# Reordering stores, weight packing, LayerNorms and product chains in a Strassen-type transformer kernel

## The chip, the cores and the metric

The kernel runs on one core of one Trainium2 chip. The metric is the device time of one execution in microseconds (us). Each execution is listed with the granted TensorE clock, the share of its full speed that TensorE was let have. A profile is of one execution; its span is some 1.7 us shorter than the time of that execution.

## The reference, cut to what matters

```python
x = A_x                                     # (1, 2048, 1024) bf16
x = x + A(layernorm(x), wqkv, wo)           # linear attention: 32 heads, phi(t) = t+1 or exp(t), num / den, then wo
x = x + B(layernorm(x), w_gate, w_up, w_down)
x = x + A(layernorm(x), wqkv, wo)           # the same weights a second time
x = x + B(layernorm(x), w_gate, w_up, w_down)

def B(x, w_gate, w_up, w_down):             # F = 3584
    return ((x @ w_gate) * (x @ w_up)) @ w_down
```

## The kernel before

All large products are Strassen-type: TensorE multiplies sums and differences of blocks, and VectorE makes those sums and combines the products. A recording helper, `P.add(engine, ...)`, puts each operation on one of five engines. **Each engine takes its operations in the order in which they are given to it**, and the semaphore waits follow from what the operations read and write. In the profile's names `arena` is the on-chip memory, `ps` a bank in which TensorE accumulates, and a name ending in `scratch` a buffer in the chip's main memory. All transfers are issued by SyncE (`sp`), so there is one in-order queue of them: a transfer that must wait for its data holds up all that stand behind it. (The prediction shows a case: eight stores are issued from 955.38 us on, and the transposes behind them only from 961.44.)

The stages, with their times before: first attention 0 to 186 us, its output stage (`y_grp`, L1232) to 241, first gate/up pass to 416, down to 501, second gate/up pass to 666, down to 753; then the same again: attention 753 to 917, output stage to 979, gate/up to 1136, down to 1224, gate/up to 1382, down to 1470. The first block must make the sums of the weights. It *packs* weight columns into a scratch buffer, makes the sums and stores them; the second block only loads them.

A gate/up pass takes 14 pairs of weight units. The order of work inside a pair is a string:

```python
ORDER0 = "D3A' P5B' R0 51 D4B' T0 P1A D3B' 56 P1B P6A R0 T1 D2A P6B P7A P5A 57 S5+ D2B P7B D4A"
ORDER1 = "D4A' P5B' 11 D3A' 51 16 D4B' D2B' T1 R0 P1A 17 D3B' P6A 56 S5+ T0 P1B 41 D2A 57 R0 P6B S2+ 46 P7A P5A 47 P7B"
```

`P1A` is product 1 of unit A on a PSUM bank, `D2`, `D3`, `D4` are last products and the multiplication, `51`, `56`, `57` are steps of a second Strassen level inside product 5, and `'` means "of the pair before". `R0` issues the next load of the ring of weight buffers. `T0` and `T1` are ticks, where other work is hooked in. `S5+` and `S2+` are the sums of weights for the next pair: the first block makes them on VectorE and stores them, the second block loads them.

The hooks that the change touches:

```python
def pack():                                  # two transfers of 256 KB, 256 bytes at a time
    ...
    for i in range(2):
        dma(w16[:, i], wgu_v[m][:, :, c0:c0 + 128], ...)

def stash(i):                                # store a part of the residual x
    dma(xscr[i * 128:(i + 1) * 128, :], x_res[:, i, :], ...)

# output stage of the attention block, item i of 16
for i in range(NST):
    ...                                      # normalization, ring loads
    nxt.b1_one()                             # LayerNorm of the next block, in steps
    y_grp(tok[i], 0, i)
    y_seed(i + 1)                            # ScalarE copies the residual into PSUM ahead of its products
    nxt.b2_one()
    y_grp(tok[i], 1, i)
    if not first and i == 9:
        for k in range(8):
            stash(k)

# second attention block: finish one LayerNorm per item from item 1 on
elif n >= 1:
    ...
    job(n, 0, lnp.flush_b)
    job(n, 2, lnp.flush_a)

# hooks of the first gate/up pass and of its down product
def ticks0(u):
    if u % 2 == 0 and not lnp.done():
        lnp.flush_step()                     # a LayerNorm
    if first and u:
        wd_tick(u)                           # down weights: load, sums, store
    if first and u % 2 == 0:
        pack()
```

## Time and profile before

| | us |
|---|---|
| time, median of 4 runs | 1478.07 (1476.38 to 1478.68) |
| span of the profile | 1473.8 |
| TensorE busy | 1442.5 (98%) |
| TensorE's starts beyond the matmuls' own pace | 42.6 |

The last row is the useful one. It is worked out in the prediction: the distance between the starts of two matmuls, less the time that the first needs at full pace. The page's part 4 follows back what released the last instruction, and who released that, as shares of the span by engine:

```profile
PE 74%; DVE 11%; DMA 9%; issue 2%; ACT 2%; POOL 1%; SPq 1%; DVEq 0%; ACTq 0%; POOLq 0%
```

A quarter of the chain that ended last is not TensorE, although TensorE is busy 98%. The view of waits says which transfers VectorE waited for (total us, how many times, the longest):

```profile
DVE arena L757 <- DMA arena<-in_B_w_down_dram: 21.3, 12, 6.7
DVE arena L757 <- DMA arena<-w_scratch: 13.7, 9, 2.3
```

The first are the down weights in the first gate/up pass, the second the ring loads in the second pass.

### The profile page before, as it was taken

What the parts mean: (1) busy time and instruction counts of PE and PEld (TensorE: products, weight loads), DVE (VectorE), ACT (ScalarE), POOL (GpSimd) and SP (SyncE); (2) the same over time, 40 slices, a digit from 0 to 9 for tenths busy, and PEclk for the clock granted to TensorE, in tenths of its full rate; (3) what the DMA queues carried; (4) which work ended last, traced back from release to release, by engine and by line L of the source; (5) the groups of instructions that cost most, each with busy time, mean ns of one, the idle gap of its engine ahead of it and who ended that gap; (6) DMA issues with size and microseconds to landing.
All of it is one profiled execution on the core that took longest, in us unless ns stands there. A gap on an engine that the chain in (4) does not pass through costs nothing.

```text
span 1473.8 us, 21078 instructions
## 1 busy us (share of the span) xinstructions
PE 1442.5 (98%) x7850; PEld 755.0 (51%) x7850; DVE 1126.3 (76%) x2248; ACT 655.9 (45%) x1354; POOL 138.9 (9%) x176
## 2 busy tenths in 40 slices
PE   8999999999999999999999999999999999999999
PEld 3444444445544466554444444446666445666544
DVE  6987878888854698887579878778888636888842
ACT  5672345444410165551037823557776004777400
POOL 2203521000000000001010045210000000000000
PEclk9999999999999999999999999999999999999999
DMA  7478966999866766777884167668775856777652
GB/s 257 87 200 229 216 135 155 276 313 305 282 219 212 244 236 236 236 254 255 269 271 129 51 171 162 170 154 275 262 259 189 305 180 218 263 263 257 211 192 96
DMA packets 270456, 320.18 MB, mean 217 GB/s; under 512 B 161936, under 2 KB 212880, under 8 KB 270352
## 3 DMA queue, kind: packets, MB, share of 16 engines
q1 hardware_dynamic: 270352, 318.82, 70.9%
q8 instruction: 62, 1.02, 0.3%
q14 instruction: 42, 0.34, 0.1%
HBM read 236.45 MB, written 73.40 MB: 210 GB/s over the span
## 4 chain that ended last, share of the span: by engine, by line
PE 74%; DVE 11%; DMA 9%; issue 2%; ACT 2%; POOL 1%; SPq 1%; DVEq 0%; ACTq 0%; POOLq 0%
PE ps L1596 23%; PE ps L1310 21%; PE ps L1391 14%; PE ps L1130 6%; PE ps L911 6%; DMA arena<-w_scratch 3%; DVE arena L757 3%; DMA arena<-arena 3%; PE ps L882 3%; DVE arena L443 2%; DMA arena<-in_B_w_down_dram 2%; DVE arena L1007 1%; SPq L416 1%; DVE arena L1004 1%; PE ps L1232 1%
## 5 line engine op out<-in xcount | busy, mean ns | idle before, releaser
L757 DVE TENSOR_TENSOR arena<-arena 128x512 f16<-128x512 f16 (+10 forms) x951 | 432.4, 480 | 96.1 <-ACT arena L1395 32.4
L760 DVE SCALAR_TENSOR_TENSOR arena<-ps,arena 128x512 f16<-128x512 f32 (+2 forms) x497 | 334.3, 686 | 175.1 <-PE ps L1596 151.3
L1310 PE MATMUL ps<-arena 128*128 128x512 f16 x1888 | 459.2, 380 | 5.6 <-DVE arena L760 5.1
L1596 PE MATMUL ps<-arena 128*128 128x512 f16 (+1 forms) x1568 | 340.9, 379 | 0.0
L1391 PE MATMUL ps<-arena 128*128 128x256 f16 x2184 | 289.8, 273 | 8.7 <-ACT arena L1395 4.8
L1310 PEld LDWEIGHTS ps<-arena 128*128 128x128 f16 (+1 forms) x1888 | 183.5, 98 | 170.3 <-DVE arena L760 9.3
L1391 PEld LDWEIGHTS ps<-arena 128*128 128x128 f16 (+1 forms) x2184 | 211.3, 98 | 102.6 <-ACT arena L1395 14.0
L1596 PEld LDWEIGHTS ps<-arena 128*128 128x128 f16 x1568 | 153.4, 98 | 183.1
L1315 ACT ACTIVATE arena<-ps 128x512 f32<-128x512 f32 x224 | 134.1, 598 | 61.4 <-PE ps L1310 49.0
L1339 ACT COPY ps<-ps 128x512 f32<-128x512 f32 x112 | 65.4, 584 | 182.2 <-PE ps L1310 172.7
L1395 ACT ACTIVATE arena<-ps 128x256 f32<-128x256 f32 x351 | 125.3, 385 | 24.4 <-PE ps L1391 20.1
L911 PE MATMUL ps<-arena 128*128 128x512 f16 (+1 forms) x560 | 123.2, 379 | 3.3 <-ACT arena L918 1.2
L1401 ACT COPY ps<-ps 128x256 f32<-128x256 f32 x182 | 65.8, 362 | 135.3 <-DVE ps L1404 73.9
L1232 PE MATMUL ps<-arena 128*128 128x512 bf16 x512 | 113.0, 383 | 4.0 <-ACT ps L1226 4.0
L1130 PE MATMUL ps<-arena 128*128 128x512 bf16 x512 | 116.1, 379 | 0.0
L443 DVE BATCH_NORM_STATS2 arena<-arena 128x6 f32<-128x512 bf16 x128 | 88.3, 689 | 11.9 <-DMA arena<-in_A_x_dram 6.9
L1013 POOL TENSOR_TENSOR arena<-arena 128x1024 f16<-128x1024 f32 x32 | 75.5, 2358 | 189.5 <-DVE arena L1011 172.2
L911 PEld LDWEIGHTS ps<-arena 128*128 128x128 f16 x560 | 53.9, 98 | 71.6 <-ACT arena L918 5.4
L882 PE MATMUL ps<-arena 128*128 128x512 bf16 x384 | 85.5, 379 | 4.0 <-ACT arena L547 1.6
L1232 PEld LDWEIGHTS ps<-arena 128*128 128x128 f16 x512 | 50.2, 99 | 66.4 <-ACT ps L1226 5.4
L446 POOL TENSOR_SCALAR arena<-arena 128x1 f32<-128x1 f32 x64 | 20.3, 317 | 659.8 <-DVE arena L445 659.8
L1404 DVE TENSOR_TENSOR ps<-ps,arena 128x256 f32<-128x256 f32 x182 | 77.8, 428 | 2.6 <-PE ps L1391 2.6
(56 smaller groups left out, 750.5 us busy)
## 6 DMA issues: line engine op xcount, KB each, us to landing
arena<-w_scratch SPq DMA_DIRECT2D x84, 896.0 KB, 4.9
arena<-t_scratch SPq DMA_DIRECT2D x32, 896.0 KB, 5.9
arena<-in_B_w_down_dram SPq DMA_DIRECT2D x24, 896.0 KB, 5.5
arena<-sp_scratch SPq DMA_DIRECT2D x26, 768.0 KB, 4.4
w_scratch<-arena SPq DMA_DIRECT2D x28, 512.0 KB, 5.6
arena<-w_scratch SPq DMA_DIRECT2D x28, 384.0 KB, 4.7
x_scratch<-arena SPq DMA_DIRECT2D x40, 256.0 KB, 7.6
arena<-x_scratch SPq DMA_DIRECT2D x40, 256.0 KB, 5.7
```

What stands on the lines that cost most here:

```text
L443: P.add("dve", (lambda h: lambda e: e.bn_stats(st[j][:, 6 * h:6 * h + 6], x_res[:, i, (D // 2) * h:(D // 2) * (h + 1)]))(h), rd=r_x(i, (D ...
L757: P.add("dve", lambda e: e.tensor_tensor(out=out, in0=a, in1=b, op=op), rd=rd, wr=wr, prd=prd)
L760: P.add("dve", lambda e: e.scalar_tensor_tensor(out=out, in0=a, scalar=sc, in1=b, op0=ALU.mult, op1=op1), rd=rd, wr=wr, prd=prd)
L882: return [e.matmul(psb(bank), xnT[:, k, i * 128:(i + 1) * 128], t[:, k, h * 512:(h + 1) * 512], start=(k == 0), stop=(k == KT - 1)) for k ...
L911: P.add("pe", lambda e: [e.matmul(psb(bank), a[0][:, k, :], b[0][:, k, :], start=(q in (1, 5) and k == 0), stop=(k == 3), skip_group_check ...
L1130: return [e.matmul(psb(bank), xrt[t][:, jj * 128:(jj + 1) * 128], pk[:, h, t, :], start=(t == tok[0]), stop=(t == tok[NST - 1])) for t in ts]
L1232: return [e.matmul(psb(bank), xnT[:, g, i * 128:(i + 1) * 128], wp[:, g, dh * 512:(dh + 1) * 512], start=(dh == 0 and g == 0), stop=(g == ...
L1310: P.add("pe", lambda e: [e.matmul(psb(bank), w[:, k, :], x[:, k, :], start=(start and k == 0), stop=(k == 3), skip_group_check=True) for k ...
L1315: P.add("act", lambda e: e.activation(t, psb(bank), AF.Copy, scale=SG), prd=[bank], wr=r)
L1391: P.add("pe", lambda e: [e.matmul(psb(bank)[:, 256 * half:256 * half + 256], w[:, k, :], xx[:, k, :], start=(start and k == 0), stop=(k == ...
L1395: P.add("act", lambda e: e.activation(d, src, AF.Copy, scale=sc), prd=[xk], wr=rd_)
L1596: P.add("pe", lambda e: [e.matmul(psb(bank), hv[:, 7 * hf + k, t * 128:(t + 1) * 128], w[:, k, :], start=(q in "15" and hf == 0 and k == 0 ...
```

## The change

The intent is to keep what TensorE waits for from standing behind late transfers. It adds and removes no matmul. The core of the diff:

```diff
-    ORDER0 = "D3A' P5B' R0 51 D4B' T0 P1A D3B' 56 P1B P6A R0 T1 D2A P6B P7A P5A 57 S5+ D2B P7B D4A"
-    ORDER1 = "D4A' P5B' 11 D3A' 51 16 D4B' D2B' T1 R0 P1A 17 D3B' P6A 56 S5+ T0 P1B 41 D2A 57 R0 P6B S2+ 46 P7A P5A 47 P7B"
+    ORDER0 = "D3A' P1A P7B' P6A D2B' 51 D4B' D3B' R0 56 D2A P1B T0 P7A 57 P5A W P6B T1 D4A R0 P5B S5+"
+    ORDER1 = "P5A' 47' T0 P7B' D4A' P5B' 11 D3A' R0 51 16 D4B' D2B' P1A 17 T1 56 D3B' P6A P1B 41 R0 57 S5+ S2+ D2A P6B 46 P7A"
 ...                                         # second attention block
-                elif n >= 1:
+                elif n >= 2:
 ...                                         # output stage
+                if first and i % 3 == 1:
+                    pack()
 ...
-                if not first and i == 9:
-                    for k in range(8):
-                        stash(k)
+                if not first and i >= 8:
+                    stash(i - 8)
 ...                                         # head of a gate/up pass
-                pre = ("P1A", "P1B") + (("P5A", "P5B") if l2 else ())
+                pre = ("P1A", "P1B") + (("D2A", "D2B") if jit else ()) + ("P5A", "P5B")
 ...
+                early = not first
+                if early:
+                    for q in "25":
+                        sums(1, q)           # the next pair's sums are loaded first of all
 ...
             def ticks0(u):
-                if u % 2 == 0 and not lnp.done():
-                    lnp.flush_step()
-                if first and u:
-                    wd_tick(u)
+                if first and u % 2:
+                    wd_next()                # sums only; the token W issues the loads and stores
                 if first and u % 2 == 0:
                     pack()

             def dticks0(q, t):
-                if q == "2" and t == 3:
-                    for k in range(8):
-                        stash(8 + k)
+                if q in "12" and not lnp.done():
+                    lnp.flush_step()         # LayerNorms now under the down product
+                if q in "26":
+                    stash(8 + 4 * "26".index(q) + t)
```

Cut here: the operand sums of the first pair are now made one per token, and `wd_tick` is split into `wd_dma` (load and store) and `wd_next` (sums).

More of the change, by code (lines that the diff above doesn't have):

```diff
@@ L1496, in gateup, with tp_next @@
                 n0 = ps_ * NPASS
-                pre = ("P1A", "P1B") + (("P5A", "P5B") if l2 else ())
+                pre = ("P1A", "P1B") + (("D2A", "D2B") if jit else ()) + ("P5A", "P5B")
                 tpl = tp_ops(ps_, l2)
-                early = [(q, f) for q in dict.fromkeys(tk[0] for tk in order if tk[0] in l2) for f in tpl[q][:3]]
-                def b12(q):
-                    for x in [x for x in early if x[0] == q]:
-                        x[1]()
-                        early.remove(x)
-                    tpl[q][3]()
+                todo = [(q, k) for q in dict.fromkeys(tk[0] for tk in order if tk[0] in l2) for k in range(4)]
+                plain = set()
+                def tp_next(q0=None):
+                    for q, k in list(todo):
+                        if (q == q0) if q0 else (k < 3 or q in plain):
+                            assert k < 3 or q in plain
+                            todo.remove((q, k))
+                            tpl[q][k]()
+                            if not q0:
+                                return
                 def emit(p, tk, head=False):
@@ L1512, in emit @@
                         return
+                    if p == 1 and tk[0] in l2 and tk[1] == "1":
+                        tp_next(tk[0])
                     c, x = pairs[p], "AB".find(tk[-1])
@@ L1522, in emit @@
                             ring_issue()
-                    elif tk[0] == "S":
+                    elif tk == "W":
+                        wd_dma()
+                    elif tk[0] == "S" and not (early and p == 0):
                         sums(p + (tk[2] == "+"), tk[1])
-                    else:
+                    elif tk[0] == "T":
                         i = int(tk[1])
@@ L1532, in emit @@
                     if p == 0 and tk in ("P1B", "P5B", "D2B", "D4B") and tk[1] in l2:
-                        b12(tk[1])
+                        plain.add(tk[1])
+                    if p == 0 and not head:
+                        tp_next()
                 if jit:
@@ L1542, in gateup @@
                         emit(p, tk)
-                        if p == 0 and early:
-                            early.pop(0)[1]()
                 late = [tk for tk in order if tk[-1] == "'"]
@@ L1642, in layer_B, with wd_dma, wd_next @@
             if first:
-                def wd_tick(u):
-                    j = u // 2
-                    if u % 2:
-                        wd_prep(j)
-                    else:
-                        if j:
-                            wd_store(j - 1)
-                        if j < NJ:
-                            wd_load(j)
+                wd = dict(load=0, prep=0, store=0)
+                def wd_dma():
+                    if wd["store"] < wd["prep"]:
+                        wd_store(wd["store"])
+                        wd["store"] += 1
+                    if wd["load"] == wd["prep"] and wd["load"] < NJ:
+                        wd_load(wd["load"])
+                        wd["load"] += 1
+                def wd_next():
+                    if wd["prep"] < wd["load"]:
+                        wd_prep(wd["prep"])
+                        wd["prep"] += 1
             def ticks0(u):
-                if u % 2 == 0 and not lnp.done():
-                    lnp.flush_step()
-                if first and u:
-                    wd_tick(u)
+                if first and u % 2:
+                    wd_next()
                 if first and u % 2 == 0:
@@ L1661, in dticks0 @@
             def dticks0(q, t):
-                if q == "2" and t == 3:
-                    for k in range(8):
-                        stash(8 + k)
+                if q in "12" and not lnp.done():
+                    lnp.flush_step()
+                if q in "26":
+                    assert q == "2" or lnp.done()
+                    stash(8 + 4 * "26".index(q) + t)
                 if q == "5":
@@ L1710, in layer_B @@
             if first:
-                wd_tick(0)
+                wd_dma()
             tail = gateup(0, ticks0, L2SETS[not first, 0])
-            if first:
-                wd_tick(2 * NJ)
-            lnp.need(NST - 1)
+            while first and wd["store"] < NJ:
+                wd_next()
+                wd_dma()
             tq = t_ops(1)
```

## The prediction

> **What bounds the kernel now.** I read the page first, part 1: TensorE is busy almost all the span.
>
> ```profile
> PE 1442.5 (98%) x7850; PEld 755.0 (51%) x7850; DVE 1126.3 (76%) x2248; ACT 655.9 (45%) x1354; POOL 138.9 (9%) x176
> ```
>
> The change alters no matmul, so the matmul work is a floor, and all there is to win is TensorE's waiting. A busy share hides short waits (a group's mean 512-column matmul "lasts" 379 ns, but in the chain of waits 378 of them take 81.58 us, 0.2158 us each), so I went through the trace's matmul start times and took 0.2158 us per 512 columns (0.109 per 256, from 14 in 1.53 us) off each step. What is left over is 42.6 us in the whole span: 10.4 us before 100 us, which the change does not touch, 1.3 at 184 us, 28.5 us in nine places after 240 us, and crumbs. That is 1.9% of 1478.1, so a gain over 2% is nearly out of reach.
>
> Then the table of stretches, cut at the stages. Its columns are the stretch, its length, busy time of PE, PEld, DVE, ACT, POOL with counts, the granted clock, the DMA share and GB/s.
>
> ```profile
> 241.00:258.00 17.00, 13.95 (x60) 5.96 (x59) 16.04 (x41) 6.55 (x12) 1.80 (x4) 0.92 0.87 236
> 306.00:330.60 24.60, 24.42 (x130) 12.41 (x129) 21.57 (x55) 11.58 (x23) 0.00 (x0) 1.00 1.01 326
> 501.00:666.50 165.50, 160.59 (x1005) 97.09 (x1004) 142.06 (x324) 98.21 (x229) 0.00 (x0) 1.00 0.73 244
> 753.50:796.00 42.50, 40.25 (x184) 17.29 (x183) 38.40 (x95) 30.08 (x56) 5.06 (x12) 1.00 0.71 203
> 917.00:979.00 62.00, 58.03 (x262) 25.56 (x260) 43.34 (x84) 32.12 (x45) 14.01 (x28) 0.97 0.65 173
> ```
>
> The first is the entry of the first gate/up pass: VectorE is busy 16.04 of 17 us and TensorE waits for it. The second lies in the same pass: DMA is full (1.01). The third is the first block's second gate/up pass, the fourth the second block's first projections, the fifth its output stage. Last, the timeline says who ends the waits (start, length, engine, line; in brackets the idle time and its releaser):
>
> ```profile
> 254.35 1.15 PE L1310 MATMUL ps<-arena 128*128 128x512 f16 x4 [2.63 <-DVE arena L760]
> ...
> 302.60 1.55 DVE L757 TENSOR_TENSOR arena<-arena 128x512 f16<-128x512 bf16 x4 [1.99 <-DMA arena<-in_B_w_down_dram]
> ...
> 588.56 1.02 DVE L757 TENSOR_TENSOR arena<-arena 128x256 f16<-128x256 f16 x4 [2.17 <-DMA arena<-w_scratch]
> ...
> 591.16 0.39 PE L1391 MATMUL ps<-arena 128*128 128x256 f16 x2 [1.12 <-ACT arena L1395]
> ...
> 761.03 0.55 DVE L463 TENSOR_SCALAR arena<-arena 128x1024 f16<-128x1024 bf16 x1 [1.55 <-DMA arena<-arena]
> ...
> 955.38 6.03 SPq L416 DMA_DIRECT2D x_scratch<-arena  x8
> 961.44 20.00 SPq L531 DMA_TRANSPOSE arena<-arena  x7
> 966.06 1.24 ACT L460 ACTIVATE arena<-arena 128x1024 f16<-128x1024 bf16 x1 [6.37 <-DMA arena<-arena]
> ...
> 968.44 10.49 PE L1232 MATMUL ps<-arena 128*128 128x512 bf16 x40 [2.36 <-ACT ps L1226]
> ...
> 1234.12 0.61 PE L1391 MATMUL ps<-arena 128*128 128x256 f16 x4 [1.81 <-DMA arena<-sp_scratch]
> ```
>
> All follow one pattern: an in-order engine (VectorE, ScalarE or the one DMA queue) is stuck on a late transfer, and what TensorE needs stands behind it.
>
> **What the Trainium skill says.** "TensorE: Matmul & The Clock Gate", section "Back-to-back issue gap": a warm matmul takes N/2.4 + 2.5 ns, 215.8 ns at 512 columns; the trace's 0.2158 us agrees. Its section "What's actually happening" says an idle window of about 3.4 us drops the array to half clock until about 3.4 us of activity. Here the waits of 2.79 us (before 254.35) and 2.53 us (before 968.44) are each followed by steps of 0.427 us, costing 1.6 us more; the wait of 1.77 us at 952.09 is not. So waits above about 2.5 us count extra. "Perfetto Trace Analysis", section "Identifying the Most-Contended Engine", warns that matmul busy share is no measure of distance to the limit; agreed, 31.3 us idle hide 42.6. "DMA: Bandwidth & Descriptors", section "Why small descriptors are slow (HBM only)", puts 27% overhead on 256-byte descriptors. The weight packing moves 128 bf16 columns at a time, that is 256 bytes; the page counts 161936 packets under 512 B, and the passes with packing are those at DMA share 1.0.
>
> **The change part by part** (waits before, my estimate after, all in us):
>
> 1. *Entry of the first gate/up pass, 5.1 to 1.8.* Before: 0.59 + 2.79 waited, 1.6 at half clock. VectorE had 16 weight-sum ops (6.06), a LayerNorm (0.54 + 1.42 + 0.21) and 8 more sums (2.98) ahead of the 0.68 us op that TensorE awaited until 254.29. The change drops the LayerNorm (2.2), puts two product groups (D2A, D2B, 2 x 0.86) ahead of P5, and puts the pair's second sums and the down sums (3.0) behind that op. It should then run near 249.5, when D3A' comes at 241.4 + 10 x 0.863 = 250.0. The next pair's step 51 then waits for about 1.5 + 1.5 + 1.0 us of sums, some 1 to 2 us.
> 2. *Down weights in that pass, 1.95 to 1.2* (0.73, 0.68, 0.34, 0.20 at 292, 305, 317, 377 us). VectorE waited 21.3 us for these loads in all. In the new order a pair's load stands behind its packing in the queue (2.5 us of issue), but the op that needs it comes 9.9 us after D3A' and not 5.5. Packing ends at pair 5, not 10, as five of 28 packs go to the output stage; from there I expect no wait. *Handover to down, 1.35 to 0.7.*
> 3. *Packing in the first output stage, 0 to 1.3, a loss.* Each of the five pairs of transfers is 0.5 MB in the same queue as the LayerNorm transposes. The one beside two ring loads (near 214 us) puts 1.3 to 2 us of issue before a transpose that now takes 5.31 us and that ScalarE already awaits (0.77 idle at 219.67). The seed copies ScalarE makes there finish only 0.2 to 0.7 us ahead of need.
> 4. *First block's second gate/up pass, 6.2 to 2.0* (eight waits of 0.26 to 1.39). The sums of the next pair wait for a ring load (13.7 us on VectorE in all), and the step behind them, 57, waits too. The new order moves these sums from 4.3 to 5.4 us after the load's issue and behind step 57. The load takes 5.9 to 7.0 us, so some wait stays.
> 5. *LayerNorm one item later, 3.0 to 1.3.* It removes VectorE's wait of 1.55 us at 761.03 and delays 2.2 us of work.
> 6. *Stores one by one, 4.1 to 0* (2.53 and 1.6 at half clock). The eight stores took the queue for 6.03 us and held up the transposes that ScalarE awaited for 6.37. The wait of 1.77 at 952 us comes from two ring loads of 0.9 MB, and stays.
> 7. *Entry of the second block's gate/up, 1.95 to 0.9.* Two LayerNorms of 2.2 us leave VectorE. But the sums' load now stands right behind the last store, whose data must be read first.
> 8. *Sums a pair ahead in the last pass, 2.8 to 2.6.* Their load already leaves at 1225.80, directly behind the last output store, and lands 8.27 us later. Issuing it "earlier" in program order changes nothing there.
>
> LayerNorms moved under down cost nothing: VectorE is busy 40.59 of 84.5 us there. Sum: 5.1 + 1.95 + 1.35 + 0 + 6.2 + 3.0 + 1.77 + 4.1 + 1.95 + 2.8 = 28.2 before (28.5 by the list of starts), 1.8 + 1.2 + 0.7 + 1.3 + 2.0 + 1.3 + 1.77 + 0 + 0.9 + 2.6 = 13.6 after: 14.6 us gained, 1478.1 to about 1463.5.
>
> **The rivals.** *The new chain is too tight.* In ORDER0 P1A follows D4A's last matmul by 1.08 us, and a 0.60 us ScalarE copy plus about 0.25 us of handover lies between; P6A follows P1A with 0.86 us for a 0.57 us copy plus the same. If either misses by 0.3 us in each of 14 pairs, 4 us go; with VectorE at 10.5 of 11.9 us a pair, a late load could add 0.5 us more a pair. That makes 1467 to 1476. Against it: the steps measured for such handovers do fit. *The packing merely moves the wait.* If the delayed transpose costs over 2.5 us, the half clock adds 1.6, and part 3 becomes 4: 1466. For it: ring loads of 0.9 MB did this at 952 us. Against: before, this stage has DMA share 0.54. *Everything fits*, and only 952 and 1234 us remain: 1454.
>
> **Range and chances.** These give 1463, 1455 to 1472. All nine waits gone would be 28.5 us, below the 29.6 us of 2%: chance 0.01 of faster. Slower by 29.6 us needs 1 us lost in every gate/up pair of the first block: 0.02.
>
> **What would show it.** Part 1: the stretch after 241 us at clock 1.00 and no wait over 2 us. Part 3: ScalarE's wait for a transpose near 220 us grown to 2 to 3 us, with a TensorE wait behind it. Part 4: VectorE's wait for the ring load falling from 13.7 us to under 8. Part 6: no ScalarE wait of 6 us and clock 1.00 in the second output stage. Part 8: a wait for the sums of 1.5 to 2 us still there near 1220 us. I am wrong if the gate/up pair in the first block takes over 12 us where it took 11.9, or if the second pass keeps its eight waits.

## More of the kernel before

The view of transfers for that second pass (525 to 650 us) has, in its first row, the busy share of the 16 DMA engines in 40 slices of 3.1 us, and further down each kind of transfer, with the median time from issue to landing:

```profile
DMA  6399479919980997189409964894299439935993
...
arena<-w_scratch SPq DMA_DIRECT2D x20, 896.0 KB, 5.8
sp_scratch<-arena SPq DMA_DIRECT2D x10, 768.0 KB, 5.5
```

18 of the 40 slices stand at 9 and 14 at 4 or less: transfers come in bunches.

## The result, and the profile after

The changed kernel took 1460.49 us (median of 4 runs, 1458.59 to 1462.22), against 1478.07 for the kernel before. The ratio is 0.9883, with a 95% interval of 0.9865 to 0.9900. A ratio here is always the mean time of one kernel's fast runs over that of the other's fast runs of the same rounds, so it is not quite the ratio of the medians. The gain is real, 17.6 us, and under 2%. The changed kernel was measured again later (`after_ref`, below); there it gained 14.9 us.

The page after, part 1 and the shares of the chain that ended last:

```profile
PE 1437.1 (99%) x7850; PEld 755.1 (52%) x7850; DVE 1133.2 (78%) x2248; ACT 657.6 (45%) x1354; POOL 144.7 (10%) x176
...
PE 86%; DVE 7%; DMA 3%; ACT 2%; issue 1%; POOL 1%; SPq 0%; ACTq 0%; DVEq 0%
```

The counts of instructions of each engine are the same. DMA's share of the chain fell from 9% to 3%. The excess of TensorE's starts, worked out as before, fell from 42.6 to 25.6 us: 17.0 us, which is the fall of the span (1473.8 to 1456.9) within 0.1. So the whole gain is TensorE waiting less.

The same stretches as in the prediction, with the same columns. The fourth begins 10 us earlier, as that stage now does:

```profile
241.00:258.00 17.00, 14.32 (x67) 5.96 (x65) 15.70 (x40) 8.55 (x13) 1.58 (x4) 1.00 0.66 180
306.00:330.60 24.60, 24.60 (x132) 12.57 (x130) 22.58 (x54) 11.85 (x25) 0.00 (x0) 1.00 0.94 304
501.00:666.50 165.50, 165.50 (x1039) 101.23 (x1038) 146.19 (x328) 97.71 (x229) 0.00 (x0) 1.00 0.71 247
...
743.50:786.00 42.50, 41.05 (x189) 17.83 (x188) 37.94 (x94) 30.96 (x57) 5.06 (x12) 1.00 0.68 192
```

TensorE starts 67 matmuls in the first stretch instead of 60, at clock 1.00 instead of 0.92, but is still not full. The second and third have no idle time left. The fourth improved by less than a microsecond. TensorE's own timeline in the second output stage (start, length, engine, line; in brackets the idle time and its releaser) shows that the wait before 968.44 is gone and the one that stood at 952 stays:

```profile
906.90 32.97 PE L1232 MATMUL ps<-arena 128*128 128x512 bf16 x152
941.45 22.62 PE L1232 MATMUL ps<-arena 128*128 128x512 bf16 x104 [1.58 <-ACT ps L1226]
```

VectorE's waits for the down weights, 21.3 us before, and those for the ring loads, 13.7 us before, have become this one line; the ring loads are no longer listed:

```profile
DVE arena L757 <- DMA arena<-in_B_w_down_dram: 0.8, 3, 0.4
```

There are also new waits. The timeline of the first output stage (SPq is the transfer queue):

```profile
213.68 1.30 SPq L416 DMA_DIRECT2D w_scratch<-in_B_w_up_dram  x2
...
215.03 8.32 SPq L531 DMA_TRANSPOSE arena<-arena  x3
...
220.85 1.24 ACT L460 ACTIVATE arena<-arena 128x1024 f16<-128x1024 bf16 x1 [2.76 <-DMA arena<-arena]
...
223.23 12.26 PE L1232 MATMUL ps<-arena 128*128 128x512 bf16 x56 [1.43 <-ACT ps L1226]
...
246.91 4.49 PE L1311 MATMUL ps<-arena 128*128 128x512 f16 x20 [1.99 <-ACT ps L1340]
```

A packing pair is issued at 213.68. The LayerNorm transposes stand behind it, ScalarE waits 2.76 us for one of them, and its seed copy comes late, so TensorE waits. The line at 246.91 is the same thing at the head of the gate/up pass. By TensorE's starts these two are 1.59 and 2.15 us; the bracket gives a little less.

### The profile page after: what moved, and what is told of

Read it like the earlier page. It is cut to its first block, busy times and chain, and to the rows that moved or that the text cites. A ratio compares the mean times of both kernels' runs of the same rounds, so it can differ in the third digit from the quotient of the medians.

```text
span 1456.9 us, 21047 instructions
## 1 busy us (share of the span) xinstructions
PE 1437.1 (99%) x7850; PEld 755.1 (52%) x7850; DVE 1133.2 (78%) x2248; ACT 657.6 (45%) x1354; POOL 144.7 (10%) x176
## 4 chain that ended last, share of the span: by engine, by line
PE 86%; DVE 7%; DMA 3%; ACT 2%; issue 1%; POOL 1%; SPq 0%; ACTq 0%; DVEq 0%
PE ps L1311 27%; PE ps L1609 23%; PE ps L1392 16%; PE ps L1130 8%; PE ps L911 6%; PE ps L882 3%; PE ps L1232 2%; DMA arena<-arena 2%; DVE arena L443 2%; DVE arena L757 1%; DVE arena L604 1%; DMA arena<-in_A_wqkv_dram 1%; POOL arena L1013 1%; DMA arena<-sp_scratch 1%; PE ps L1156 0%
## 5 line engine op out<-in xcount | busy, mean ns | idle before, releaser
L1311 PE MATMUL ps<-arena 128*128 128x512 f16 x1888 | 457.3, 379 | 2.7 <-ACT ps L1340 2.0
L1311 PEld LDWEIGHTS ps<-arena 128*128 128x128 f16 (+1 forms) x1888 | 182.8, 98 | 165.6 <-ACT ps L1340 6.3
L1405 DVE TENSOR_TENSOR ps<-ps,arena 128x256 f32<-128x256 f32 x182 | 76.7, 428 | 10.5 <-PE ps L1392 9.6
```

The source lines that it names most:

```text
L1311: P.add("pe", lambda e: [e.matmul(psb(bank), w[:, k, :], x[:, k, :], start=(start and k == 0), stop=(k == 3), skip_group_check=True) for k ...
```

## The experiments

Twelve kernels ran, in four calls; each call has its own runs of the kernel before (medians 1474.74, 1476.44, 1475.70 and 1473.05 us, on three chips), so ratios are compared across calls rather than times. All experiments but two (`order1_only`, `late_ln_only`) start from the changed kernel. A line of code can have a number one or two higher or lower from kernel to kernel: L1309, L1310 and L1311 are the same matmul.

### Is packing in the output stage a gain or a loss?

`no_pack` takes it out; the packing then happens in the gate/up pass as before. `pack_early` does the same five packings, but all before the LayerNorm transposes begin.

```diff
-                if first and i % 3 == 1:         # no_pack: these two lines removed
-                    pack()
+                if first and i < 2:              # pack_early, in their place
+                    for _ in range(3 - i):
+                        pack()
```

> The changed kernel without the five packings in the first output stage. Theory (the packing delays the LayerNorm transposes there, ScalarE and VectorE fall behind, and the three waits of the changed kernel at 223, 236 and 247 us, 1.59 + 0.78 + 2.15 us, are one cause): all three gone or under 0.5 us each, first gate/up entry before 240 us. Packing then runs to pair 10 of the first gate/up pass. If the new chain order alone cured that pass, it stays without waits between 260 and 415 us and the kernel is about 4 us faster than the changed one, 1456. Rival (the packing moved away is what cured the pass): 1 to 2 us of waits for the down weights come back there, and the total is 1458 to 1460. Second rival (the wait at 247 us comes from the LayerNorms moved, not from packing): it stays, total 1458.

> The changed kernel with the same five packings in the first two iterations of the output stage, before any LayerNorm transpose is issued. Theory: the waits at 223, 236 and 247 us go (4.5 us) and the gate/up pass stays clean: about 1456. Rival (any packing in this stage costs, by its bytes): half of the waits stay, 1458.

`no_pack` took 1454.96 us (1454.48 to 1455.16), ratio 0.9872 (0.9857 to 0.9888); `pack_early` 1455.72 us, ratio 0.9878 (0.9862 to 0.9894). Later the changed kernel itself, `after_ref`, had 0.9902 (0.9886 to 0.9918), so leaving the packing out is worth 4.4 us by these two ratios, and 4.5 by the waits that went (against 0.9883 of the first runs it is 1.6, with intervals that overlap). TensorE's timeline in `no_pack`:

```profile
208.81 31.93 PE L1232 MATMUL ps<-arena 128*128 128x512 bf16 x146
240.57 6.21 PE L1309 MATMUL ps<-arena 128*128 128x512 f16 x28
247.47 6.22 PE L1309 MATMUL ps<-arena 128*128 128x512 f16 x28 [0.69 <-ACT arena L1314]
```

One unbroken row of 146 matmuls stands where the changed kernel had waits at 223 and 236 us, and the wait of 2.15 us at the head of the pass is gone with them. Only the 0.69 remains (0.85 by the starts). The gate/up pass behind it has no TensorE wait over 0.2 us although it packs five units more. The rival, that packing in the output stage relieves the pass, falls: this part is a net loss, by what it does to the transposes. `pack_early` confirms that it is the place in the queue that costs and not the work.

### What cleaned the first gate/up pass?

`order0_old` puts the old ORDER0 back into the changed kernel, with the new token W ahead of T0. `order0_exact` does so with the down-weight transfers where they were.

```diff
-    ORDER0 = "D3A' P1A P7B' P6A D2B' 51 D4B' D3B' R0 56 D2A P1B T0 P7A 57 P5A W P6B T1 D4A R0 P5B S5+"
+    ORDER0 = "D3A' P5B' R0 51 D4B' W T0 P1A D3B' 56 P1B P6A R0 T1 D2A P6B P7A P5A 57 S5+ D2B P7B D4A"   # order0_old
+    # order0_exact: the same without W, and wd_dma() called in ticks0 ahead of pack()
```

> The changed kernel with the chain order of before in the first gate/up pass, the down-weight transfer issued just ahead of the packing as before. Theory (the distance of 9.9 us in place of 5.5 us from the issue to the use of the down weights is what cured this pass): VectorE waits again 10 us or more for the down weights in all, and TensorE waits again 2 to 3.3 us between 260 and 420 us: total 1462 to 1464. Rival (LayerNorms gone from the pass and less packing cured it): under 1 us of waits there, total as changed, 1460.

`order0_old`: 1460.32 us, ratio 0.9908 (0.9889 to 0.9927). A wait of 2.24 us came back at 257 us, but nothing between 260 and 420 us, and VectorE's waits for down weights were only 3.8 us, all in one wait. As the order and the place of the transfers had both changed, this did not tell the theories apart.

> The changed kernel with the chain order of the first gate/up pass of before and the down-weight transfers at exactly the place of before, between the weight-sum store and the packing. (The earlier try put them ahead of that store.) Theory (queue place and distance to the use cured the waits for the down weights): VectorE waits again 8 us or more for these loads before packing ends, TensorE 1 to 2 us between 260 and 420 us. Rival (the LayerNorms gone from VectorE in the first three pairs, or shorter transfer times with less packing, cured it): VectorE waits under 4 us, TensorE under 0.3 us. In both cases the wait of about 2.2 us at the entry, near 257 us, is back as in the earlier try.

`order0_exact`: 1462.98 us (1460.64 to 1464.28), ratio 0.9908 (0.9888 to 0.9928), against 0.9902 for `after_ref`. VectorE's waits for down weights are back almost in full, 18.9 us in 13 waits, and yet TensorE lost only 0.42 us at 258 (where I had expected 2.2 again) and 0.88 at 415, nothing between. The line in `order0_old`, then in `order0_exact`:

```profile
DVE arena L757 <- DMA arena<-in_B_w_down_dram: 3.8, 1, 3.8
DVE arena L757 <- DMA arena<-in_B_w_down_dram: 18.9, 13, 6.3
```

Both have the old order, and they differ in the place of the down-weight transfers alone: ahead of the weight-sum store or behind it. So it is the place in the queue, and not the new order, that cures most of **VectorE's** wait. For TensorE the new order and place together save the 0.42 and 0.88 us, and the new order brings a wait of 0.85 us at 252 us: some 0.5 us net. The 1.95 us in that pass were cured by something else. `late_ln_only` is the test: the kernel before, with nothing changed but the LayerNorms moved out of the pass and under the down product.

```diff
 def ticks0(u):
-    if u % 2 == 0 and not lnp.done():
-        lnp.flush_step()
 def dticks0(q, t):
+    if q in "12" and not lnp.done():
+        lnp.flush_step()
```

> The kernel before with only the last LayerNorms moved from the gate/up pass to the down stage behind it. Theory (VectorE's slack decides whether a late down-weight load reaches TensorE): VectorE still waits 15 us or more for down weights, but TensorE's waits between 286 and 400 us (1.95 us in the profile of before) fall under 0.7, the one at the first block's entry falls from 2.8 us to under 1.5, and the two of 1.0 and 0.3 us at 990 us in the second block go: 1472 to 1474 where before is 1477. Rival (the queue place is what counts): waits between 286 and 400 us stay over 1.2 us.

It took 1469.5 us (1464.71, 1470.95, 1474.3 and 1468.06; a wide spread), ratio 0.9959 (0.9936 to 0.9983). Its waits for down weights and its first stretch:

```profile
DVE arena L757 <- DMA arena<-in_B_w_down_dram: 17.9, 12, 6.3
...
241.00:258.00 17.00, 15.97 (x77) 7.09 (x76) 16.59 (x44) 7.15 (x14) 0.68 (x2) 1.00 0.81 249
```

VectorE waits 17.9 us and TensorE starts 77 matmuls in the first stretch (60 before): the entry cost 0.55 + 0.80 us instead of 5.1, and the waits between 286 and 400 us are gone. With the LayerNorms away VectorE has enough slack to wait for the down weights without passing it on. The handover to down keeps 0.94 us, so that is not the LayerNorms' doing. At the second block's entry the waits of 1.04 and 0.31 us went, as expected, but one of 0.80 us stands at 972 us, so that 1.65 of 1.95 us remain. The time came out below the 1472 to 1474 that I expected. The share of ORDER0 itself, some 0.5 us net, is read from comparing profiles only, since the times do not resolve it.

### What cleaned the second gate/up pass?

`order1_only` is the kernel before with the new ORDER1 and nothing else.

> The kernel before with only the new chain order of the first block's second gate/up pass. Theory (the order alone moves the sums of the next pair behind step 57 and away from the ring load): the eight waits of 6.2 us between 560 and 660 us go, nothing else changes: 1472. Rival (the late LayerNorms and spread stores shape the transfers there too): 2 us or more of waits stay, 1474 or more.

It took 1465.44 us (1464.93 to 1467.3), ratio 0.9946 (0.9929 to 0.9963). All eight waits between 560 and 660 us are gone, and no wait of VectorE for a ring load is left:

```profile
501.00:666.50 165.50, 165.50 (x1039) 101.29 (x1037) 146.28 (x327) 97.68 (x229) 0.00 (x0) 1.00 0.70 248
```

This part alone does it. The gain by the ratio is 8 us (5.5 to 10.5), and the waits that went sum to 6.2; in this run the waits of the first pass also happened to be smaller than in the first profile of before (a wait of 2.79 us stood there too, but without the half clock behind it).

But why? I had expected the ring load to take as long as before. The transfers of the changed kernel in the same stretch:

```profile
DMA  8677577856876785688568866856885688665869
...
arena<-w_scratch SPq DMA_DIRECT2D x19, 896.0 KB, 4.6
sp_scratch<-arena SPq DMA_DIRECT2D x11, 768.0 KB, 3.2
```

One slice at 9 and none under 5. The same load lands in 4.6 us instead of 5.8, the same store in 3.2 instead of 5.5. The issues explain the difference: before, a pair's two stores and two loads left at 576.82, 577.19, 579.15 and 581.61 us, within 4.8 us, then none for 8 us. In the changed kernel they leave over 8.6 us. `order1_bunch` tests this by moving one token: the second ring load goes behind the stores.

```diff
-    ORDER1 = "... P6A P1B 41 R0 57 S5+ S2+ D2A P6B 46 P7A"
+    ORDER1 = "... P6A P1B 41 57 S5+ S2+ R0 D2A P6B 46 P7A"
```

> The changed kernel with one token of the second gate/up pass moved: the second ring load of a pair is issued behind the two stores of the sums instead of ahead of step 57, so that two stores (256 and 768 KB) and two loads (896 KB each) leave within about 5 us, as in the kernel before (4.8 us), instead of within about 9. Everything else as in the changed kernel. Theory A (a ring load lands late because the other three transfers share the 16 DMA engines with it): over 525 to 650 us the median landing of the ring loads rises from 4.6 us to 5.5 or more, the DMA row gets slices at 9 and slices under 4 again (before: 18 and 14 of 40; changed kernel: 1 and 0), VectorE waits for these loads again, 2 to 12 us in all, and TensorE loses 0 to 4 us: 1460 to 1465. Theory B (the loads land sooner for a reason that is not their neighbours in the queue): landing stays 4.4 to 4.8 us, the DMA row stays even, no wait for the loads on VectorE, the time within 1 us of the changed kernel's 1460.5 to 1461.6.

It took 1470.51 us (1466.66 to 1473.29), ratio 0.9979 (0.9960 to 0.9998): the one token gives back 11 to 14 us by the ratios (0.9979 against 0.9902 and 0.9883), more than the whole part was worth and more than theory A had allowed (1460 to 1465). Transfers over 525 to 650 us, then the queue's own timeline and VectorE's wait:

```profile
DMA  9249926980698049905990699069903992599169
...
arena<-w_scratch SPq DMA_DIRECT2D x20, 896.0 KB, 6.8
```

```profile
580.56 2.32 SPq L416 DMA_DIRECT2D sp_scratch<-arena  x2
582.92 1.99 SPq L416 DMA_DIRECT2D arena<-w_scratch  x2
592.85 2.32 SPq L416 DMA_DIRECT2D sp_scratch<-arena  x2
595.21 0.43 SPq L416 DMA_DIRECT2D arena<-w_scratch  x1
```

```profile
DVE arena L757 <- DMA arena<-w_scratch: 14.6, 11, 2.2
```

The bunches are back, and the landing rises to 6.8 us: theory A holds for the landing, and theory B falls. VectorE's waits, too, are over what A had allowed (2 to 12 us). The timeline also shows what theory A had missed. The loads stand behind the stores of the sums, these behind the sums, and the sums behind the loads before. That is a **closed loop** through the in-order queue, and the turn shown is 595.21 - 582.92 = 12.29 us, against 11.49 us a pair in the changed kernel (ring loads at 577.19 and 588.68). The nine turns from 533.30 to 644.98 us last 11.7 to 13.35 us, 12.4 on average, so thirteen cost some 12 us. The moved token also issues the load later: this run does not tell how much of the loss is the longer landing and how much the later issue. The kernel before has the same order of issue (store, load, store, load), and I read it as having sat at the edge of this loop, with waits in some pairs only; no run shows that by itself.

### The stores, and the LayerNorms one item later

`undo_two` puts the burst of eight stores and the old start of the LayerNorms (`n >= 1`) back; `after_ref` is the changed kernel again, in the same call.

> The changed kernel itself, unaltered, so that the runs of this call have it on the same chip. Expected: its ratio to the kernel before again between 0.9865 and 0.99, its waits at the same places as in its first profile (223, 236, 247, 777 to 792, 941 and 1217 us).

> The changed kernel with two parts undone that act at different places: the eight stores in one burst again, and the LayerNorm flush of the second block again from the first item on. Theory: the burst brings back one wait of about 2.5 us near 957 us with half clock behind it (4.1 us together), and the wait for a ring load near 941 us stays as it is; the flush brings VectorE's wait of 1.5 us for a transpose back near 747 us, but TensorE's waits between 765 and 795 us grow only from 2.4 to 3.0 us, since VectorE is over its capacity there in both. Together 4.7 us slower than the changed kernel. Rival for the LayerNorms (the item's delay gives nothing): no growth.

`after_ref`: 1461.58 us (1459.36 to 1463.62). `undo_two`: 1466.02 us (1463.84 to 1468.14), ratio 0.9930 (0.9913 to 0.9948). Undoing the two costs 4.4 us, 4.1 by the ratios. The timeline of `undo_two`:

```profile
958.13 1.24 ACT L460 ACTIVATE arena<-arena 128x1024 f16<-128x1024 bf16 x1 [6.22 <-DMA arena<-arena]
...
960.51 5.75 PE L1232 MATMUL ps<-arena 128*128 128x512 bf16 x18 [2.20 <-ACT ps L1226]
```

In the queue the stores are issued from 947.60 on and the transposes only from 953.49; ScalarE waits 6.22 us, as before the change. 18 matmuls take 5.75 us here: seven of them start 0.427 us apart, at half clock. The LayerNorm waits of the second attention block were 2.9 us in `undo_two` and 2.3 in `after_ref`; the stores are nearly all of the gain.

These runs also show that one and the same wait is followed by the half clock in one run and not in another. The head of the gate/up pass has the same wait of 2.15 us in `order0_exact` and in `after_ref`; here are 4.8 us that begin about at its end in each, the clock being the number before the last two:

```profile
248.50:253.30 4.80, 4.80 (x15) 1.88 (x16) 4.66 (x13) 1.06 (x2) 0.21 (x1) 0.64 0.73 218
```

```profile
246.70:251.50 4.80, 4.48 (x20) 1.85 (x20) 4.66 (x13) 1.37 (x3) 0.24 (x1) 1.00 0.72 214
```

15 matmuls against 20, for the same wait. One such episode costs about 1.5 us, a good part of the 4 us over which the runs of one kernel spread. "TensorE: Matmul & The Clock Gate", section "What's actually happening", says that the window of activity is 3413 ns long and runs free of the kernel's start. The traces agree: in each of them all changes of the granted clock lie whole multiples of 3.413 us apart (in the kernel before at 255.15, 258.56, 968.53 and 971.94 us). With the traces cut at these multiples, what decides is the waiting inside one window. Between 60 and 1440 us of the 14 traces, all seven windows with 2.15 us or more of TensorE's waiting were followed by the half clock, and no window with 2.08 us or less was. The wait of `order0_exact`, 246.31 to 248.46, lies whole in the window from 246.24 to 249.66; the same wait of `after_ref`, 244.54 to 246.69, is cut by a boundary at 245.47 into 0.93 and 1.22 us. What is left to chance is where the boundaries fall.

### Towards a better version

`best` leaves the packing out, issues the ring loads of the output stage at items 6 and 10, loads the last pass's first sums earlier, and finishes the LayerNorms only in every second item.

```diff
-                elif n >= 2:
+                elif n >= 2 and (n % 2 == 0 or n > 10):
-                elif RG["n"] < NR:
+                elif RG["n"] < NR and i in (6, 10):
+                if is_last and q == "3" and t == 0:      # in the down product ahead of the last pass
+                    sp_load(1, 1, "2")
```

> The changed kernel with four places mended: no packing in the output stage; the last two ring loads at iterations 6 and 10 of an output stage, not 6 and 7; in the last block the first load of the sums issued at the start of the last down product, ahead of its last two ring loads; the second block's LayerNorms at every second item. Theory: waits at 223, 236, 247 us go (4.5), the one at 941 us goes (1.7), the one at 1217 us goes (1.1 to 2.1; the two after it of 0.2 and 0.65 stay), those between 765 and 795 us shrink from 2.4 to under 1: about 8 us faster than the changed kernel, ratio to before near 0.983. Rival for the sums (they land late because the DMA engines are busy, wherever they stand): the wait at 1217 us stays over 1 us. Rival for the LayerNorms (spread out they meet the buffers that later items use): waits move to 795 to 850 us and stay 2 us.

It was **wrong** (relative error 0.105), so its 1453.94 us count for nothing as a version. The LayerNorm of item 10 wrote a buffer that other work takes over from item 9 on; the hand-over had to move with it, and with the hand-over moved, in `best3`, the result is right. Two readings of its profile are of use. The wait for the sums near 1217 us is gone, and the wait of 1.69 us for the transposes near 937 us is not: items 6 and 10 are the wrong place for the ring loads.

`best2` has the ring loads at items 11 and 14 and the LayerNorms as in the change. `best3` is `best2` with the LayerNorms in every second item and the hand-over at item 12.

```diff
+                elif RG["n"] < NR and (first or i in (11, 14)):      # best2, best3
+                elif n >= 2 and (n % 2 == 0 or n > 10):              # best3
+                    if n == 12:                                      # hand-over of the buffer, was n == 9
```

> The changed kernel with three places mended and the LayerNorms left as the change has them: no packing in the output stage; the last two ring loads of the second block's output stage at iterations 11 and 14 in place of 6 and 7; the first load of the sums for the last pass issued at the start of the last down product. Correct again, which clears these three of the wrong result of the try before. Theory: the waits at 223, 236, 247 us and the one at 1217 us are gone as in that try, and the one at 941 us goes too, because ScalarE has caught up by iteration 11: about 8 us faster than the changed kernel's 1461.6 beside it, ratio to before 0.984. Rival: the wait comes from any 0.9 MB load among the transposes, and moves by four iterations: ratio 0.985.

> The same with the second block's LayerNorms at every second item, and the spare buffer that they write handed to the projections at item 12, not 9. Theory: the wrong result of the try before came from that hand-over, so this one is correct; VectorE's load is evened out and the four waits between 765 and 795 us (2.3 us) fall under 1 us in all. Rival: VectorE is over capacity wherever they stand, and 2 us stay, spread to 830 us.

`best2`: correct, 1453.5 us (1451.47 to 1455.17), ratio 0.9850 (0.9836 to 0.9864). `best3`: correct, **1451.29 us** (1449.93 to 1453.05), ratio 0.9837 (0.9823 to 0.9850), better than both kernels. In the changed kernel the sums' load stood behind the output store, three in a row, and TensorE waited:

```profile
1209.74 1.51 SPq L416 DMA_DIRECT2D arena<-sp_scratch  x3
...
1217.19 0.60 PE L1392 MATMUL ps<-arena 128*128 128x256 f16 x4 [0.95 <-DMA arena<-sp_scratch]
```

In `best2` the same step, at 1212.63 us, has no idle time before it. And in `best3` the first projections and the output stage of the second block, by the same columns as above, are full but for 0.28 us (just behind the first stretch, at 786 and 798 us, waits of 0.34 and 0.38 us remain):

```profile
739.50:782.00 42.50, 42.50 (x199) 19.09 (x198) 37.75 (x93) 32.34 (x59) 3.16 (x8) 1.00 0.68 185
904.50:966.50 62.00, 61.72 (x289) 27.86 (x288) 48.77 (x98) 37.01 (x52) 14.85 (x30) 1.00 0.72 185
```

## Why the prediction was right or wrong

The prediction was right, 1463 against 1460.5, and in the main for the reason that it gave: TensorE's waits are all there is to win, they are in nine places, and in-order engines that are held up cause them. "All follow one pattern", a late transfer, was too wide: in the first gate/up pass and at its entry the LayerNorms in VectorE's queue decided whether TensorE waited, as `late_ln_only` shows. The nearness of the total is in part luck: parts 1, 3 and 5 kept 3.6 us more than predicted, parts 2, 4 and 8 kept 4.5 us less. Step by step, in us, after being the first profile:

| part | before | predicted | after |
|---|---|---|---|
| 1 entry of the first gate/up pass | 5.1 | 1.8 | 3.2 |
| 2 down weights in it, handover to down | 3.3 | 1.9 | 0 |
| 3 packing in the output stage | 0 | 1.3 | 2.4 |
| 4 second gate/up pass | 6.2 | 2.0 | 0 |
| 5 LayerNorm one item later | 3.0 | 1.3 | 2.4 |
| ring loads in the second output stage | 1.77 | 1.77 | 1.74 |
| 6 stores one by one | 4.1 | 0 | 0 |
| 7 entry of the second block's gate/up | 1.95 | 0.9 | 0.85 |
| 8 sums in the last pass | 2.8 | 2.6 | 2.0 |
| sum | 28.2 | 13.6 | 12.6 |

Outside these places the wait at 184 us fell from 1.27 to 0.5. That is chance: no kernel here changes the code before it, and the waits there went from 0.17 us (`late_ln_only`) to 1.12 + 1.32 us (`best2`). What is left of the 17.0 us is smaller than that.

**Part 6** held to the number, and `undo_two` shows it. **Part 7** held as well, but the LayerNorms' leaving, which it named as the cause, left 1.65 us there in `late_ln_only`; what took the rest is open. **Part 8** was sized from one profile: its first wait is 1.11 us in the first profile of the changed kernel, under the 1.5 to 2 that the prediction looked for, and 2.08 in the second, where this place cost 2.9 in all. The stated reason, the load's place behind the output store, is shown by `best2`.

**Part 4** was mis-sized, and the term is "The load takes 5.9 to 7.0 us, so some wait stays". I took the landing time as a property of the load. It is a property of the order that I was about to change: 5.8 us at the median in the old bunches, 4.6 in the new order, 6.8 in `order1_bunch`. "DMA: Bandwidth & Descriptors", section "Issuing engines are not separate DMA queues", says that all transfers, whichever engine starts them, run on the same 16 DMA engines and interleave; the longer landings beside the uneven DMA rows fit that, though no run shows the interleaving itself. One issue in the new order lands in 577.19 to 581.62 and the sums start at 582.75, so 2.0 us of waiting became 0.

**Parts 1 and 3** belong together, and I split them wrongly. The entry's mechanism (LayerNorm and sums ahead of the awaited operation) was right: `late_ln_only` takes it to 1.35, `no_pack` to about 1. What I had missed is that packing reaches beyond its stage: its late transposes delay the ScalarE work at the head of the pass, 2.15 us, a wait that I had foreseen in neither part, and by which the sign for part 1, "no wait over 2 us", failed; the wait of 1 to 2 us on VectorE's sums that I did foresee there did not come. Counted with its cause, packing costs 4.5 instead of 1.3 us. That is the rival "The packing merely moves the wait", at the size I gave it (4), but without the half clock that I had thought necessary for it.

**Part 2** ended better than predicted, for a reason that I had only half: I gave the cure to the shorter packing and to the later need. `late_ln_only` and `order0_exact` show that the LayerNorm's removal from VectorE's queue is enough for TensorE inside the pass, even while VectorE waits 18 us. The handover to down is another matter: 0.94 and 0.88 us of it stayed in these two runs, and it went in `order0_old`, with the new place of the transfers.

**Part 5** was too hopeful by 1.1: the delayed work still meets the projections one item later. Spread over every second item, in `best3`, it leaves 0.7.

The rule "waits above about 2.5 us count extra" was wrong in kind: 2.15 us was followed by half clock in three profiles and not in three others, a wait of 2.79 us once each way. What counts is the waiting inside one window of 3.413 us, as worked out above.

The rival "The new chain is too tight" did not come true: a pair of the first pass has no TensorE wait over 0.2 us. Open stay the 0.85 us at the entry of the first pass, which a copy of ScalarE's ends in the versions with the new ORDER0, and the exact share of ORDER0.

## What to carry to other kernels

When TensorE is 98% busy, list its waits one by one and ask of each which late transfer an in-order engine is stuck on; the cure is to change who stands ahead of whom, and in the DMA queue a small urgent transfer should not stand behind large ones that can wait. Landing times read from a profile belong to that profile's order of issue: look at the row of DMA shares before using them, and keep loads from standing behind stores of results that need the loads before them, since that closes a loop. A new place for background transfers must be judged also by the stage behind it.

## What the Trainium skill lacked or had wrong

- "TensorE: Matmul & The Clock Gate", section "What's actually happening", names an idle window of about 3.4 us for the drop to half clock. Here the window did not have to be idle throughout: seven windows of 3.413 us with 2.15 to 2.62 us of waiting were followed by it, at about 1.5 us each, and none with 2.08 us or less. The page gives the free-running window but not how much of it must be idle.
- The same page, section "Back-to-back issue gap", gives the N/2.4 + 2.5 ns that the prediction used for a single, isolated matmul, and about 131 ns for a 512-column matmul in a stream. Here the stream itself took 0.2158 us a matmul.
- "DMA: Bandwidth & Descriptors" has no figure for how the landing of a whole load grows with its neighbours in the same queue. The same 896 KB load took 4.6, 5.8 or 6.8 us at the median by the order of issue alone, and the same 768 KB store 3.2 or 5.5.
- No page has the closed loop of load, sums, store and next load through one in-order queue: 12.4 us a turn on average, where a pair otherwise took 11.49, and 11 to 14 us of the whole time for one token moved.
